# Attention and two expert layers: high parts copied from the operand tiles, loads three heads ahead, transfers and scaling in another order

## The chip, the cores and the metric

One core of a Trainium2 chip. TensorE (PE) multiplies, VectorE (DVE), ScalarE (ACT) and GpSimd (POOL) work element by element, and SyncE (SP) issues all of this kernel's transfers, one after the other. The metric is the time of one execution in microseconds; lower is better.

## The reference

Three stages on float32 data: block-causal attention over 4 batches of 8 heads, 576 positions of 64; a layer g = h cos(h) between two products; and eight experts mixed by a matrix that 8 rounds of row and column scaling make from logits.

```python
scores = scale * np.matmul(q, k.transpose(0, 1, 3, 2))
...
scores = np.where(mask, scores, -1000000000.0)
scores = scores - np.max(scores, axis=-1, keepdims=True)
attn = np.exp(scores)
attn = attn / (np.sum(attn, axis=-1, keepdims=True) + 1e-09)
return np.matmul(attn, v).astype(np.float32)
...
h = x @ w_in
g = h * np.cos(h)
return (g @ w_out).astype(np.float32)
...
for e in range(E):
    h = np.maximum(x @ w1[e], 0.0)
    ye = h @ w2[e]
    out += P[:, e:e + 1] * ye
```

## The kernel before, in words

The order of every engine's queue is the order in which the code is written. `attention()` runs a loop over the 32 heads (batch and head); the two expert stages follow and are not touched.

Precision comes from splitting a float32 value into a high part (rounded to the type fp32r that TensorE reads in one pass) and a low part, the rest. A head i has its K and Q in one tile `st` (K in rows 0 to 63, Q in rows 64 to 127). The scores of a head are sums of two products. One has the high parts: `KA` and `QA` hold them in rows 0 to 63, and in rows 64 to 100 the mask and the row maxima. The other has 128 rows: `KB` holds K's low part and, below it, K's high part; `QB` holds Q's high part and, below it, Q's low part. There are two of each (j = i % 2). The steps for a head:

- `load` fetches `st` (two buffers) by two transfers, `load_v` fetches V by two.
- `hi` copies on ScalarE: K's high part into `KA`, Q's into `QA`, and both into `HI`, a single tile.
- `lo` subtracts on GpSimd: `KB` = `st` - `HI` (both low parts).
- `move_q` and `move_k` are transfers that move halves to the other rows: Q's low part from `KB` to `QB`, Q's high part from `HI` to `QB`, K's high part from `HI` to `KB` (over the low part of Q that the first one has read).
- `peak` (two halves) multiplies high parts for the row maxima, which VectorE reduces out of the PSUM tile `px` (one buffer); `turn` transposes them and `maxima` writes them into `QA`. This is done one head ahead.
- `weights` (four parts) makes the scores and ScalarE their exps; `pv` (five parts) multiplies them with V, into the PSUM tile `o` (one buffer). A column of ones in V gives the sums of the exps.
- `evac` copies `o` out on ScalarE (L338) into one of four tiles (`tla`, `raw`, `tt`), and writes the row of sums to memory (`sums`).
- For each pair of heads e, e + 1: `fetch` reads the sums back as a small tile `sc`, `invert` takes the reciprocal on VectorE and writes it to memory (`inv`), `spread` reads it into `RB` over 64 rows, twice (the transfers tt<-inv), `scale` multiplies on GpSimd, and `x_hi` (ScalarE) and `x_lo` (GpSimd) split the result into the next stage's input.

In 27 heads of 32 (`work`: all but every sixth) five steps of `conv_gen` are put in between, which turn 64-bit weights into float32: a load of 512 KB (`cw`), VectorE's L94, L113, L117 and L124, ScalarE's L100 and L101, GpSimd's L126.

A transfer waits at SyncE until what it reads is made and what it overwrites is free, and all transfers behind it wait as well.

Of the kernel before, what the change touches and what calls it, by code (L numbers as in the profile page):

```python
# [10 lines left out]
F32 = mybir.dt.float32  # L11
# [4 lines left out]
AF = mybir.ActivationFunctionType  # L16
ALU = mybir.AluOpType
# [23 lines left out]
def attention_moe_kernel(ctx: ExitStack, tc: tile.TileContext, qk, v, w_a, gate, w_b, out):  # L41
    nc = tc.nc
# [107 lines left out]
    def attention():  # L150
        with tc.tile_pool(name="at1", bufs=1) as p1, tc.tile_pool(name="at2", bufs=2) as p2, \
# [3 lines left out]
            NH = B * H  # L155
# [8 lines left out]
            HI = p1.tile([128, S], F32R, name="hi")  # L164
# [17 lines left out]
            def some(n):  # L182
                for _ in range(n):
                    next(conv_gen, None)

            def load(i):
                st[i] = p2.tile([128, S], F32, tag="st", name="st")
                nc.sync.dma_start(out=st[i][0:64, :], in_=qk[i][0:64, 1, :])
                nc.sync.dma_start(out=st[i][64:128, :], in_=qk[i][64:128, 0, :])
# [28 lines left out]
                nc.vector.memset(V[1][:, :, 0:D], 0.0)  # L218
                nc.vector.memset(V[1][:, :, 0:1], 1.0)

            def hi(i):
                j = i % 2
                nc.scalar.activation(KA[j][0:64, :], st[i][0:64, :], AF.Copy)
                nc.scalar.activation(QA[j][0:64, 64:640], st[i][64:128, :], AF.Copy)
                nc.scalar.activation(HI, st[i], AF.Copy)  # L225

            def lo(i):

                nc.gpsimd.tensor_tensor(out=KB[i % 2], in0=st[i], in1=HI.bitcast(F32), op=ALU.subtract)  # L229

            def move_q(i):
                j = i % 2
                nc.sync.dma_start(out=QB[j][64:128, :].bitcast(F32), in_=KB[j][64:128, :].bitcast(F32))
                nc.sync.dma_start(out=QB[j][0:64, :].bitcast(F32), in_=HI[64:128, :].bitcast(F32))

            def move_k(i):
                nc.sync.dma_start(out=KB[i % 2][64:128, :].bitcast(F32), in_=HI[0:64, :].bitcast(F32))

            def first_head():

# [9 lines left out]
            def peak(i, u):  # L250

                q, k, nm = QA[i % 2], KA[i % 2], NM[i % 2]
                ps = psx.tile([128, 1024], F32, tag="x", name="px")

                def part(t, k0, n, at):
                    nc.tensor.matmul(ps[:, at:at + n], q[0:68, 128 * t:128 * t + 128], k[0:68, k0:k0 + n],  # L256
                                     start=True, stop=True)

                if u == 0:
                    part(4, 320, 256, 256)  # L260
                    part(3, 0, 448, 0)
                    part(4, 0, 512, 512)
                    found = ((3, 0, 448), (4, 448, 576))
                else:
                    part(1, 0, 256, 0)
                    part(2, 0, 320, 192)
                    part(0, 0, 256, 512)
                    found = ((1, 0, 192), (2, 192, 320), (0, 512, 64))
                for t, at, n in found:
                    nc.vector.tensor_reduce(out=nm[:, 96 + t:97 + t], in_=ps[:, at:at + n], op=ALU.max, axis=AX.X)  # L270
# [42 lines left out]
            def pv(i, c):  # L313
                m = D + 1 if i % 2 == 0 else 2 * D
                if c == 0:
                    ps_o[i] = pso.tile([128, 1024], F32, tag="o", name="o")
                o = ps_o[i][0:m]
                vt = V[i % 2][:, :, 0:m]
                if c == 0:
                    nc.tensor.matmul(o[:, 512:1024], vt[:, 0], EP.pop(i), start=True, stop=True)  # L320
                    nc.tensor.matmul(o[:, 448:512], vt[:, 0], EQ[i][:, 0:64], start=True, stop=True)
                elif c == 1:
                    nc.tensor.matmul(o[:, 576:1024], vt[:, 1], EQ.pop(i)[:, 64:512], start=False, stop=True,
                                     skip_group_check=True)
                elif c == 2:
                    nc.tensor.matmul(o[:, 704:1024], vt[:, 2], ER[i][:, 0:320], start=False, stop=True,
                                     skip_group_check=True)
                elif c == 3:
                    nc.tensor.matmul(o[:, 832:1024], vt[:, 3], ER.pop(i)[:, 320:512], start=False, stop=True,
                                     skip_group_check=True)  # L330
                else:
                    nc.tensor.matmul(o[:, 960:1024], vt[0:64, 4], EC.pop(i), start=False, stop=True,
                                     skip_group_check=True)

            def evac(i):
                m = D + 1 if i % 2 == 0 else 2 * D
                t = RAW[i // 2 % 2][i % 2]
                nc.scalar.activation(t[0:m], ps_o.pop(i)[0:m, 448:1024], AF.Identity, bias=eps[0:m, i % 2:i % 2 + 1])  # L338
                if i % 2 == 0:
                    SUMS[i] = dr.tile([2, S], F32, tag="s", name="sums")  # L340
                s = SUM[i % 2]
                nc.sync.dma_start(out=SUMS[i - i % 2][i % 2:i % 2 + 1, :], in_=t[s:s + 1, :])

            def fetch(e):
                nc.sync.dma_start(out=SC, in_=SUMS.pop(e).rearrange("h (p j) -> p h j", j=8))

            def invert(e):
                nc.vector.reciprocal(out=SC, in_=SC)
                INV[e] = dr.tile([2, S], F32, tag="i", name="inv")
                nc.sync.dma_start(out=INV[e].rearrange("h (p j) -> p h j", j=8), in_=SC)  # L350

            def spread(e):
                d = INV.pop(e)
                for h in range(2):
                    nc.sync.dma_start(out=RB[64 * h:64 * h + 64, :], in_=d[h:h + 1, :].partition_broadcast(64))
# [2 lines left out]
                b, p = divmod(e // 2, NC)  # L358
                return p, slice(b * S, (b + 1) * S)

            def scale(e):
                for h in range(2):
                    r = slice(64 * h, 64 * h + 64)
                    nc.gpsimd.tensor_tensor(out=XF[r, :], in0=RAW[e // 2 % 2][h][r, :], in1=RB[r, :], op=ALU.mult)

            def x_hi(e):
                nc.scalar.activation(xh[:, place(e)[0], place(e)[1]], XF, AF.Copy)

            def x_lo(e):
                p, cols = place(e)  # L370
                nc.gpsimd.tensor_tensor(out=xl[:, p, cols], in0=XF, in1=xh[:, p, cols].bitcast(F32),
                                        op=ALU.subtract)
# [8 lines left out]
            peak(0, 1)  # L381
            turn(0)
            maxima(0)
            hi(1)
            lo(1)
            for i in range(NH):
                nxt, even, odd = i + 1 < NH, i % 2 == 0, i % 2 == 1
                work = i % 6 != 5
                if even and i >= 4:
                    scale(i - 4)  # L390
                if odd and i >= 5:
                    x_lo(i - 5)
                if i:
                    evac(i - 1)
                if nxt:
                    move_q(i + 1)
                if i and nxt:
                    load_v(i + 1)
                if i + 2 < NH:
                    load(i + 2)  # L400
                if nxt:
                    peak(i + 1, 0)
                weights(i, 0)
                weights(i, 1)
                weights(i, 2)
                weights(i, 3)
                if odd and i >= 3:
                    invert(i - 3)
                if work:
                    some(2)  # L410
                if nxt:
                    peak(i + 1, 1)
                pv(i, 0)
                pv(i, 1)
                if nxt:
                    turn(i + 1)
                    maxima(i + 1)
                for c in range(2, 5):
                    pv(i, c)
                if nxt:  # L420
                    move_k(i + 1)
                if even and i >= 2:
                    fetch(i - 2)
                if odd and i >= 3:
                    spread(i - 3)
                if work:
                    some(1)
                if i + 2 < NH:
                    hi(i + 2)
                    lo(i + 2)  # L430
                if work:
                    some(2)
                if even and i >= 4:
                    x_hi(i - 4)
            evac(NH - 1)
            e = NH - 2
            scale(e - 2)
            return conv_gen, {0: lambda: (x_hi(e - 2), fetch(e)),
                              1: lambda: (invert(e), x_lo(e - 2)), 2: lambda: spread(e),
                              4: lambda: (scale(e), x_hi(e)), 5: lambda: x_lo(e)}  # L440

    with tc.manual_schedule():
        conv_gen, leftover = attention()
# [477 lines left out]
```

## Time and profile before

| | us |
|---|---|
| median of 3 runs | 2354.38 (2353.14 to 2354.81) |
| the profiled execution | 2354.91 |
| its span, first to last instruction | 2353.1 |
| TensorE busy | 2202.4 (94%) |
| VectorE, ScalarE, GpSimd busy | 1521.5, 1033.8, 1062.9 |

The shares are averages over the whole span. The attention heads lie in the first 370 us, where the page's slices show TensorE busy for five to seven tenths; behind that nine tenths and more.

### The profile page before, as it was taken

Reading aid. Unit: us, or ns where it says so; the run is one execution under the profiler, and the core shown is the slowest. Engines: PE = TensorE matmul, PEld = TensorE weight load, DVE = VectorE, ACT = ScalarE, POOL = GpSimd, SP = SyncE. Lnnn points to the kernel's source line nnn. Section 1 sums busy time; section 2 is a strip of 40 time slices with the busy share of each in tenths; the row PEclk is TensorE's granted clock in tenths of the full one; section 3 lists DMA queues with packets and bytes.
Section 4 is the critical chain, followed back from the end, with each engine's and each line's share of the span. In section 5 each row is a group of like instructions: output and inputs, shape, how many; then the busy total and the mean of one; then the engine's idle time right before and its main releaser. Section 6 shows DMA issues by size and latency. Waiting matters only on the chain.

```text
span 2353.1 us, 29528 instructions
## 1 busy us (share of the span) xinstructions
PE 2202.4 (94%) x10869; PEld 1945.1 (83%) x10869; DVE 1521.5 (65%) x2442; ACT 1033.8 (44%) x1912; POOL 1062.9 (45%) x897
## 2 busy tenths in 40 slices
PE   5777667999999989999999999999999999999999
PEld 4555456999899878888888888888888888888888
DVE  5445447667666677666667766666667666666665
ACT  4555545555555433343334434433443443344332
POOL 2444437666556434334435533443347444334432
PEclk9778878999999999999999999999999999999999
DMA  4454542000000112112211221221221222122211
GB/s 123 123 134 129 137 123 80 1 1 1 1 1 19 36 54 72 63 63 72 72 61 65 90 71 65 72 72 58 68 72 64 89 72 72 57 70 72 72 56 44
DMA packets 75152, 156.89 MB, mean 67 GB/s; under 512 B 31904, under 2 KB 31904, under 8 KB 75008
## 3 DMA queue, kind: packets, MB, share of 16 engines
q1 hardware_dynamic: 75008, 155.02, 21.5%
q8 instruction: 85, 1.39, 0.2%
q14 instruction: 59, 0.48, 0.1%
HBM read 136.40 MB, written 4.87 MB: 60 GB/s over the span
## 4 chain that ended last, share of the span: by engine, by line
PE 60%; DVE 4%; ACT 1%; issue 0%; DVEq 0%; ACTq 0%
PE acc L449 11%; PE acc L451 11%; PE acc L450 11%; PE hx L451 5%; PE hx L449 5%; PE hx L450 5%; PE hy L449 3%; PE hy L451 3%; PE hy L450 3%; PE hz L449 1%; PE hz L451 1%; PE hz L450 1%; DVE hl L779 1%; DVE wal L551 0%; ACT hh L778 0%; DVE wbl L540 0%
## 5 line engine op out<-in xcount | busy, mean ns | idle before, releaser
L560 POOL TENSOR_TENSOR wv<-stg,wv 128x512 fp32r<-128x512 f32 x190 | 335.5, 1787 | 856.6 <-ACT wv L559 843.1
L449 PE MATMUL acc<-wv,hh 128*128 128x512 f32 x1152 | 456.2, 396 | 0.0
L451 PE MATMUL acc<-wv,hl 128*128 128x512 f32 x1152 | 455.5, 395 | 0.0
L450 PE MATMUL acc<-wv,hh 128*128 128x512 f32 x1152 | 454.5, 394 | 0.0
L807 DVE SCALAR_TENSOR_TENSOR oa<-acc,P,oa 128x512 f32<-128x512 f32 x540 | 378.9, 740 | 4.9 <-PE acc L451 4.3
L778 ACT ACTIVATE hh<-c 128x384 fp32r<-128x384 f32 x288 | 151.2, 525 | 420.0 <-DVE c L863 170.0
L70 POOL TENSOR_TENSOR jl<-raw,jh 128x512 fp32r<-128x512 f32 x190 | 253.2, 1344 | 170.7 <-ACT jh L67 170.6
L779 DVE SCALAR_TENSOR_TENSOR hl<-c,hh 128x384 fp32r<-128x384 f32 x288 | 167.4, 581 | 176.4 <-ACT hh L778 176.4
L451 PEld LDWEIGHTS acc<-wv,hl 128*128 128x128 f32 x1152 | 216.0, 187 | 53.7
L450 PEld LDWEIGHTS acc<-wv,hh 128*128 128x128 f32 x1152 | 215.9, 187 | 44.0
L449 PEld LDWEIGHTS acc<-wv,hh 128*128 128x128 f32 x1152 | 216.1, 188 | 43.2
L857 DVE TENSOR_TENSOR c<-hz,c 128x384 f32<-128x384 f32 x96 | 53.4, 557 | 193.9 <-PE hz L451 193.9
L551 DVE TENSOR_TENSOR wal<-s,wah 128x1024 fp32r<-128x1024 f32 x96 | 172.3, 1794 | 0.0
L847 ACT ACTIVATE c<-hx 128x384 f32<-128x384 f32 x96 | 47.4, 494 | 276.6 <-PE hx L451 276.6
L270 DVE TENSOR_REDUCE nm<-px 128x1 f32<-128x448 f32 (+4 forms) x160 | 69.6, 484 | 148.2 <-PE px L256 148.1
L67 ACT ACTIVATE jh<-raw 128x512 fp32r<-128x512 f32 x192 | 119.4, 623 | 98.8 <-PE acc L450 85.1
L229 POOL TENSOR_TENSOR kb<-st,hi 128x576 fp32r<-128x576 f32 x31 | 48.3, 1558 | 208.2 <-ACT hi L225 164.3
L451 PE MATMUL h<-xh,jl 128*128 128x384 f32 x384 | 131.2, 342 | 10.5 <-POOL jl L70 10.3
L449 PE MATMUL h<-xh,jh 128*128 128x384 f32 x384 | 130.3, 339 | 6.5 <-ACT jh L67 6.3
L660 DVE TENSOR_TENSOR hl<-g,hh 128x384 fp32r<-128x384 f32 x96 | 99.6, 1038 | 56.7 <-ACT hh L658 56.7
L449 PE MATMUL acc<-hh,jh 128*128 128x384 f32 x384 | 129.8, 338 | 5.9 <-DVE xl L678 5.0
L449 PE MATMUL hy<-xh,wah 128*128 128x384 f32 x384 | 129.4, 337 | 3.8 <-DVE c L863 3.7
(211 smaller groups left out, 5311.3 us busy)
## 6 DMA issues: line engine op xcount, KB each, us to landing
stg<-in_w_b_dram SPq DMA_DIRECT2D x192, 512.0 KB
cw<-in_w_a_dram SPq DMA_DIRECT2D x32, 512.0 KB
st<-in_qk_dram SPq DMA_DIRECT2D x64, 144.0 KB
tt<-inv SPq DMA_DIRECT2D x32, 144.0 KB
out_dram<-oa SPq DMA_DIRECT2D x18, 256.0 KB
qb<-kb SPq DMA_DIRECT2D x31, 144.0 KB
qb<-hi SPq DMA_DIRECT2D x31, 144.0 KB
kb<-hi SPq DMA_DIRECT2D x31, 144.0 KB
```

What stands on the lines that cost most here:

```text
L67: nc.scalar.activation(hi, src, AF.Copy)
L70: eng_lo.tensor_tensor(out=lo, in0=src, in1=hi.bitcast(F32), op=ALU.subtract)
L270: nc.vector.tensor_reduce(out=nm[:, 96 + t:97 + t], in_=ps[:, at:at + n], op=ALU.max, axis=AX.X)
L449: nc.tensor.matmul(ps, lh, rh, start=first, stop=False, skip_group_check=go_on)
L450: nc.tensor.matmul(ps, lh, rl, start=False, stop=False, skip_group_check=go_on)
L451: nc.tensor.matmul(ps, ll, rh, start=False, stop=last, skip_group_check=go_on)
L551: eng.tensor_tensor(out=self.al, in0=self.s, in1=self.ah.bitcast(F32), op=ALU.subtract)
L560: eng.tensor_tensor(out=t[:, DM:2 * DM], in0=src, in1=t[:, 0:DM].bitcast(F32), op=ALU.subtract)
L660: nc.vector.tensor_tensor(out=G[n][1], in0=g, in1=G[n][0].bitcast(F32), op=ALU.subtract)
L778: nc.scalar.activation(hh, src, AF.Relu)
L779: nc.vector.scalar_tensor_tensor(out=hl, in0=src, scalar=0.0, in1=hh.bitcast(F32), op0=ALU.max, op1=ALU.subtract)
L807: nc.vector.scalar_tensor_tensor(out=o, in0=acc, scalar=p, in1=o, op0=ALU.mult, op1=ALU.add)
```

## The change

`hi` becomes `hi_q` (ScalarE: `HI`, then `QA`) and `hi_k` (VectorE: `KA`). `move_q` and `move_k` read the high parts from `QA` and `KA` instead of `HI`. `load` runs three heads ahead instead of two and stands behind the second peaks; `hi_q`, `hi_k` and `lo` of head i + 2 stand ahead of the products with V instead of behind them. `move_k` stands ahead of the first peaks, `sums` is parted from `evac`, `give` (the write of `inv`) from `invert`, which now opens an odd head. `scale` does one half in an even and the other in an odd head, and `x_hi` and `x_lo` follow in the odd head.

```diff
--- before.py
+++ after.py
@@ -218,11 +218,12 @@
                 nc.vector.memset(V[1][:, :, 0:D], 0.0)
                 nc.vector.memset(V[1][:, :, 0:1], 1.0)
 
-            def hi(i):
-                j = i % 2
-                nc.scalar.activation(KA[j][0:64, :], st[i][0:64, :], AF.Copy)
-                nc.scalar.activation(QA[j][0:64, 64:640], st[i][64:128, :], AF.Copy)
+            def hi_q(i):
                 nc.scalar.activation(HI, st[i], AF.Copy)
+                nc.scalar.activation(QA[i % 2][0:64, 64:640], st[i][64:128, :], AF.Copy)
+
+            def hi_k(i):
+                nc.vector.tensor_copy(out=KA[i % 2][0:64, :], in_=st[i][0:64, :])
 
             def lo(i):
 
@@ -231,10 +232,10 @@
             def move_q(i):
                 j = i % 2
                 nc.sync.dma_start(out=QB[j][64:128, :].bitcast(F32), in_=KB[j][64:128, :].bitcast(F32))
-                nc.sync.dma_start(out=QB[j][0:64, :].bitcast(F32), in_=HI[64:128, :].bitcast(F32))
+                nc.sync.dma_start(out=QB[j][0:64, :].bitcast(F32), in_=QA[j][0:64, 64:640].bitcast(F32))
 
             def move_k(i):
-                nc.sync.dma_start(out=KB[i % 2][64:128, :].bitcast(F32), in_=HI[0:64, :].bitcast(F32))
+                nc.sync.dma_start(out=KB[i % 2][64:128, :].bitcast(F32), in_=KA[i % 2][0:64, :].bitcast(F32))
 
             def first_head():
 
@@ -336,9 +337,11 @@
                 m = D + 1 if i % 2 == 0 else 2 * D
                 t = RAW[i // 2 % 2][i % 2]
                 nc.scalar.activation(t[0:m], ps_o.pop(i)[0:m, 448:1024], AF.Identity, bias=eps[0:m, i % 2:i % 2 + 1])
+
+            def sums(i):
+                t, s = RAW[i // 2 % 2][i % 2], SUM[i % 2]
                 if i % 2 == 0:
                     SUMS[i] = dr.tile([2, S], F32, tag="s", name="sums")
-                s = SUM[i % 2]
                 nc.sync.dma_start(out=SUMS[i - i % 2][i % 2:i % 2 + 1, :], in_=t[s:s + 1, :])
 
             def fetch(e):
@@ -346,6 +349,8 @@
 
             def invert(e):
                 nc.vector.reciprocal(out=SC, in_=SC)
+
+            def give(e):
                 INV[e] = dr.tile([2, S], F32, tag="i", name="inv")
                 nc.sync.dma_start(out=INV[e].rearrange("h (p j) -> p h j", j=8), in_=SC)
 
@@ -358,10 +363,9 @@
                 b, p = divmod(e // 2, NC)
                 return p, slice(b * S, (b + 1) * S)
 
-            def scale(e):
-                for h in range(2):
-                    r = slice(64 * h, 64 * h + 64)
-                    nc.gpsimd.tensor_tensor(out=XF[r, :], in0=RAW[e // 2 % 2][h][r, :], in1=RB[r, :], op=ALU.mult)
+            def scale(e, h):
+                r = slice(64 * h, 64 * h + 64)
+                nc.gpsimd.tensor_tensor(out=XF[r, :], in0=RAW[e // 2 % 2][h][r, :], in1=RB[r, :], op=ALU.mult)
 
             def x_hi(e):
                 nc.scalar.activation(xh[:, place(e)[0], place(e)[1]], XF, AF.Copy)
@@ -381,35 +385,53 @@
             peak(0, 1)
             turn(0)
             maxima(0)
-            hi(1)
+            hi_q(1)
+            hi_k(1)
             lo(1)
+            load(2)
             for i in range(NH):
                 nxt, even, odd = i + 1 < NH, i % 2 == 0, i % 2 == 1
                 work = i % 6 != 5
-                if even and i >= 4:
-                    scale(i - 4)
-                if odd and i >= 5:
-                    x_lo(i - 5)
+                if odd and i >= 3:
+                    invert(i - 3)
+                if i >= 4:
+                    scale(i - 4 - i % 2, i % 2)
                 if i:
                     evac(i - 1)
                 if nxt:
                     move_q(i + 1)
+                if odd and i >= 3:
+                    give(i - 3)
                 if i and nxt:
                     load_v(i + 1)
-                if i + 2 < NH:
-                    load(i + 2)
+                if i:
+                    sums(i - 1)
                 if nxt:
+                    move_k(i + 1)
                     peak(i + 1, 0)
                 weights(i, 0)
                 weights(i, 1)
                 weights(i, 2)
                 weights(i, 3)
-                if odd and i >= 3:
-                    invert(i - 3)
                 if work:
                     some(2)
                 if nxt:
                     peak(i + 1, 1)
+                if i + 3 < NH:
+                    load(i + 3)
+                if even and i >= 2:
+                    fetch(i - 2)
+                if odd and i >= 3:
+                    spread(i - 3)
+                if i + 2 < NH:
+                    hi_q(i + 2)
+                    hi_k(i + 2)
+                    lo(i + 2)
+                if work:
+                    some(1)
+                if odd and i >= 5:
+                    x_hi(i - 5)
+                    x_lo(i - 5)
                 pv(i, 0)
                 pv(i, 1)
                 if nxt:
@@ -417,27 +439,16 @@
                     maxima(i + 1)
                 for c in range(2, 5):
                     pv(i, c)
-                if nxt:
-                    move_k(i + 1)
-                if even and i >= 2:
-                    fetch(i - 2)
-                if odd and i >= 3:
-                    spread(i - 3)
-                if work:
-                    some(1)
-                if i + 2 < NH:
-                    hi(i + 2)
-                    lo(i + 2)
                 if work:
                     some(2)
-                if even and i >= 4:
-                    x_hi(i - 4)
             evac(NH - 1)
             e = NH - 2
-            scale(e - 2)
-            return conv_gen, {0: lambda: (x_hi(e - 2), fetch(e)),
-                              1: lambda: (invert(e), x_lo(e - 2)), 2: lambda: spread(e),
-                              4: lambda: (scale(e), x_hi(e)), 5: lambda: x_lo(e)}
+            sums(NH - 1)
+            scale(e - 2, 0)
+            scale(e - 2, 1)
+            return conv_gen, {0: lambda: (x_hi(e - 2), fetch(e)), 1: lambda: (invert(e), give(e), x_lo(e - 2)),
+                              2: lambda: spread(e), 4: lambda: (scale(e, 0), scale(e, 1), x_hi(e)),
+                              5: lambda: x_lo(e)}
 
     with tc.manual_schedule():
         conv_gen, leftover = attention()
```

SyncE's queue in one odd head of the steady state (names: `sc8` is the small tile of sums, `st` K and Q of a head, `cw` the weights to convert, `tt_117` the spread reciprocals). Before:

```order
L342 DMA sums_1562<-tla_119 1x576
L233 DMA qb0_106<-kb0_108 64x576
L234 DMA qb0_106<-hi_110 64x576
L194 DMA v0_114<-in_v_dram 128x4x64
L195 DMA v0_114<-in_v_dram 64x64
L188 DMA st_1568<-in_qk_dram 64x576
L189 DMA st_1568<-in_qk_dram 64x576
L350 DMA inv_1602<-sc8_122 72x2x8
L89 DMA cw_121<-in_w_a_dram 128x1024
L237 DMA kb0_108<-hi_110 64x576
L355 DMA tt_117<-inv_1602 64x576 x2
```

With the change, from the read of the sums at the end of the even head to the end of the odd one:

```order
L348 DMA sc8_122<-sums_1429 72x2x8
L234 DMA qb0_106<-kb0_108 64x576
L235 DMA qb0_106<-qa0_102 64x576
L355 DMA inv_1566<-sc8_122 72x2x8
L194 DMA v0_114<-in_v_dram 128x4x64
L195 DMA v0_114<-in_v_dram 64x64
L345 DMA sums_1570<-tla_119 1x576
L238 DMA kb0_108<-ka0_104 64x576
L89 DMA cw_121<-in_w_a_dram 128x1024
L188 DMA st_1614<-in_qk_dram 64x576
L189 DMA st_1614<-in_qk_dram 64x576
L360 DMA tt_117<-inv_1566 64x576 x2
```

The row of sums and the move into `kb` have changed places with the loads of `st`: `kb` now stands ahead of `cw`, the loads behind it; `inv` stands between the moves of Q and the loads of V, three transfers behind the read `sc8` on which it depends.

ScalarE's queue from one evacuation to the next, before:

```order
L338 ACTIVATE tt_116<-o_1324,eps_70 128x576
L294 ACTIVATE ep_1365<-sp_1362 128x512
L300 ACTIVATE eq_1372<-sq_1367 128x512
L306 ACTIVATE er_1379<-sr_1374 128x512
L311 ACTIVATE ec_1384<-sc_1381 64x64
L100 ACTIVATE tla_119<-tla_119,e_max_74 128x512
L101 ACTIVATE tla_119<-tla_119,e_all_76 128x512
L223 ACTIVATE ka0_104<-st_1353 64x576
L224 ACTIVATE qa0_102<-st_1353 64x576
L225 ACTIVATE hi_110<-st_1353 128x576
L367 ACTIVATE xh_78<-tt_118 128x576
L338 ACTIVATE tla_119<-o_1397,eps_70 65x576
```

With the change:

```order
L339 ACTIVATE tt_116<-o_1336,eps_70 128x576
L295 ACTIVATE ep_1365<-sp_1362 128x512
L301 ACTIVATE eq_1372<-sq_1367 128x512
L307 ACTIVATE er_1379<-sr_1374 128x512
L312 ACTIVATE ec_1384<-sc_1381 64x64
L222 ACTIVATE hi_110<-st_1323 128x576
L223 ACTIVATE qa0_102<-st_1323 64x576
L100 ACTIVATE tla_119<-tla_119,e_max_74 128x512
L101 ACTIVATE tla_119<-tla_119,e_all_76 128x512
L339 ACTIVATE tla_119<-o_1407,eps_70 65x576
```

The copy into `KA` is gone, the copies into `hi` and `qa` stand straight behind the four exps, and `xh` is in every odd head instead of every even one.

VectorE's queue around the reciprocal, before:

```order
L117 SCALAR_TENSOR_TENSOR raw_1115<-cw_121,raw_1115 128x512
L270 TENSOR_REDUCE nm0_111<-px_1130 128x1 x2
L348 RECIPROCAL sc8_122<-sc8_122 72x16
L124 SCALAR_TENSOR_TENSOR tla_119<-cw_121,tla_119 128x512
L94 TENSOR_SCALAR tla_119<-cw_121 128x512
L270 TENSOR_REDUCE nm0_111<-px_1167 128x1 x3
L278 TENSOR_TENSOR qa0_102<-pt_1178,diag_113 5x640
L113 TENSOR_SCALAR raw_1115<-cw_121 128x512
L117 SCALAR_TENSOR_TENSOR raw_1115<-cw_121,raw_1115 128x512
```

With the change:

```order
L113 TENSOR_SCALAR raw_1117<-cw_121 128x512
L117 SCALAR_TENSOR_TENSOR raw_1117<-cw_121,raw_1117 128x512
L351 RECIPROCAL sc8_122<-sc8_122 72x16
L271 TENSOR_REDUCE nm0_111<-px_1132 128x1 x2
L124 SCALAR_TENSOR_TENSOR tla_119<-cw_121,tla_119 128x512
L94 TENSOR_SCALAR tla_119<-cw_121 128x512
L271 TENSOR_REDUCE nm0_111<-px_1166 128x1 x3
L226 CAST ka1_105<-st_1097 64x576
L279 TENSOR_TENSOR qa0_102<-pt_1190,diag_113 5x640
L113 TENSOR_SCALAR raw_1117<-cw_121 128x512
```

The reciprocal has moved ahead of the two reductions of the first peaks, and the cast into `ka` stands between the reductions of the second peaks and the product that writes the maxima.

## Rows read from the trace of the kernel before

**Rows 1.** Windows: stretch, us, busy PE, PEld, DVE, ACT, POOL; clock, DMA share, GB/s.

```profile
23.53:353.69 330.16, 235.91 (x902) 167.55 (x902) 148.50 (x285) 168.95 (x294) 132.01 (x92) 0.80 0.49 129
...
373.50:455.00 81.50, 73.29 (x393) 70.68 (x392) 62.05 (x93) 45.50 (x79) 61.50 (x43) 0.96 0.10 30
```

**Rows 2.** Timeline of ScalarE, first and thirtieth evacuation: start, length, engine, line.

```profile
23.53 0.72 ACT L338 ACTIVATE tla<-o,eps 65x576 f32<-65x576 f32 x1
...
353.69 0.72 ACT L338 ACTIVATE raw<-o,eps 128x576 f32<-128x576 f32 x1
```

**Rows 3.** Waits of the engines from 23.53 to 353.69: total us, times, longest.

```profile
ACT ka L223 <- DMA st<-in_qk_dram: 71.2, 29, 4.1
...
ACT hi L225 <- DMA kb<-hi: 39.4, 17, 3.9
```

**Rows 4.** Waits of the transfer queue in the same stretch.

```profile
SPq L342 <- ACT tla L338: 83.6, 15, 8.6
```

**Rows 5.** Timeline of one head with a load of weights.

```profile
216.09 0.72 ACT L338 ACTIVATE raw<-o,eps 128x576 f32<-128x576 f32 x1
...
216.83 0.22 SPq L342 DMA_DIRECT2D sums<-raw  x1
...
217.71 0.48 SPq L233 DMA_DIRECT2D qb<-kb  x1
...
222.09 0.48 SPq L237 DMA_DIRECT2D kb<-hi  x1
222.63 0.55 SPq L345 DMA_DIRECT2D sc<-sums  x1
...
226.66 0.68 ACT L225 ACTIVATE hi<-st 128x576 fp32r<-128x576 f32 x1 [2.07 <-DMA kb<-hi]
...
227.82 0.73 ACT L338 ACTIVATE tla<-o,eps 65x576 f32<-65x576 f32 x1
```

**Rows 6.** Timeline of the head before it, which has no load of weights.

```profile
213.16 0.48 SPq L237 DMA_DIRECT2D kb<-hi  x1
...
215.50 0.69 ACT L225 ACTIVATE hi<-st 128x576 fp32r<-128x576 f32 x1
```

**Rows 7.** Timeline of the first head: GpSimd's subtraction and VectorE's two copies.

```profile
7.82 1.40 POOL L247 TENSOR_TENSOR qb<-st,hi 64x576 fp32r<-64x576 f32 x1
...
8.14 1.39 DVE L242 CAST ka<-st 64x576 fp32r<-64x576 f32 x1
...
9.56 0.46 DVE L243 CAST qa<-st 64x576 fp32r<-64x576 f32 x1
```

**Rows 8.** Timeline of SyncE in the next head, which has inv and tt.

```profile
229.70 0.49 SPq L233 DMA_DIRECT2D qb<-kb  x1
...
234.50 0.49 SPq L237 DMA_DIRECT2D kb<-hi  x1
235.82 1.24 SPq L355 DMA_DIRECT2D tt<-inv  x2
```

**Rows 9.** Timeline of SyncE and VectorE: a read of the sums behind a load of weights.

```profile
357.78 0.54 SPq L89 DMA_DIRECT2D cw<-in_w_a_dram  x1
358.41 0.46 SPq L237 DMA_DIRECT2D kb<-hi  x1
358.96 0.51 SPq L345 DMA_DIRECT2D sc<-sums  x1
...
362.94 0.25 DVE L348 RECIPROCAL sc<-sc 72x16 f32<-72x16 f32 x1 [0.40 <-DMA sc<-sums]
```

**Rows 10.** Issues of the page: the sizes of the loads.

```profile
cw<-in_w_a_dram SPq DMA_DIRECT2D x32, 512.0 KB
st<-in_qk_dram SPq DMA_DIRECT2D x64, 144.0 KB
```

**Rows 11.** Window of the head from 353.69 to 360.75, columns as in rows 1.

```profile
353.69:360.75 7.06, 7.02 (x30) 4.96 (x28) 5.52 (x9) 4.64 (x9) 6.70 (x5) 0.76 0.67 160
```

**Rows 12.** one conversion step of VectorE (tile tla): count, ns min/median/max, first and last start.

```profile
L94 DVE TENSOR_SCALAR tla<-cw x30: 408/422/1646, 18.6 to 393.0; 128x512 int32<-128x512 int32 x30
```

## The prediction

> **What bounds the kernel now.** I read the windows by stage first [rows 1]. The 32 heads fill the first 370 us of 2353. In them TensorE is 71% busy (235.9 of 330.2 us) at a granted clock of 0.80; behind them, in the first expert stage, it is 90% busy at 0.96. The change touches the heads alone, and the order of TensorE's own instructions is the same, so the question is the time from one head to the next. The evacuation of a head's output (L338) marks the heads: the first starts at 23.53, the thirtieth at 353.69 [rows 2], so 330.16 / 29 = **11.38 us a head**. No engine is that busy: by the same window a head costs TensorE 8.1, ScalarE 5.8, VectorE 5.1 and GpSimd 4.6 us. So the heads wait on a loop, and the waits name it [rows 3]: ScalarE's copy into HI waits for the transfer kb<-hi, and its first copy for the load of st. The queue of transfers waits 83.6 us for the evacuations of the even heads alone [rows 4].
>
> The loop in one head, in order of time [rows 5]: the evacuation at 216.09 releases sums at 216.83; behind it SyncE issues qb, qb, v, v, st, st, cw, and at 222.09 kb<-hi. HI may be overwritten only once that transfer has read it: the copy starts at 226.66, 4.6 us later. The copy of xh and the next evacuation (227.82) stand behind it on ScalarE. Sum: 0.74 to sums, 0.88 to the first qb, 4.4 to kb, 4.6 until kb landed, 1.15 to the evacuation = 11.7 us. Where a head has no weight to convert, no cw stands ahead of kb, which then frees HI after 2.3 us [rows 6]. So a cw ahead costs a transfer 2.3 us.
>
> **The change part by part.**
> *The source of the moves.* qb and kb are now read from QA and KA, so nothing waits for kb to overwrite HI: only GpSimd's subtraction reads HI. The 4.6 us leave the loop. The new writes of KA and QA wait for transfers issued a head earlier, and for scores that stand ahead of them anyway.
> *Loads three heads ahead, high parts behind the exps.* st is loaded a head before it is wanted; its wait (71 us [rows 3]) goes. ScalarE runs two copies for three.
> *The K copy on VectorE.* It saves ScalarE 0.68 us a head. The trace has such a copy twice: 1.39 us while GpSimd runs and 0.46 us alone [rows 7]. I take 0.9; both are below what VectorE has free, so it costs nothing by itself. The Trainium skill ("SBUF — State Buffer", Who interferes with whom) says that a VectorE copy in its two-port mode and GpSimd lock each other out for a whole instruction; the two rows agree, and by it the copy would be worth 1.39 us, and the denser stage would stretch VectorE's other work too (a rival, below).
> *Scaling over two heads, x_hi and x_lo later.* Same work, in smaller pieces. GpSimd's 4.6 us and ScalarE's 5.1 us (5.8 less 0.68) cover it in a head of 7 us or more.
> *The order of transfers.* This decides what is next. SyncE issues one transfer after the other. From the rows, a head that ends in sc takes 0.24 + 0.1 for sums and 217.71 to 223.18 for the rest, 5.8 us; a head with inv and tt takes 0.34, then 229.70 to 234.99, then 1.24 + 0.05, 6.9 us [rows 5, 8]. So **12.7 us of issuing for two heads**, and the change keeps all of it. Two waits come on top.
>
> 1. The read of the sums (sc) now stands behind cw and two st, last in its head, and the reciprocal with its inv is asked for at the very start of the next one, behind two qb. In the trace sc was issued 1.18 us after a cw with one kb between, and the reciprocal could start 3.98 us after the issue [rows 9]. Now 0.74 us more pass after cw (the two st), and one transfer of 144 KB more is ahead: by 2.3 us for cw's 512 KB [rows 10] that is 0.65. So sc lands after 3.9. With the reciprocal (0.25 [rows 9]) SyncE could issue inv 4.2 us after sc; sc and two qb fill 1.8. It waits **2.4 us in every second head**, and v, v, sums, kb, cw, st, tt all stand behind.
> 2. kb must wait until the first qb has read KB. Between them stand qb, v, v, sums: 2.7 us of issue. A qb with nothing ahead lands in 2.3; behind cw, two st and two tt it is later: at 2.3 us per 512 KB those need 2.3 + 4 x 0.65 = 4.9 us and 3.25 of issue have passed, so 3.95, a wait of 1.25. The other bound is nothing. I take **0.8 once in two heads**; where inv waits, qb has long landed.
>
> 12.7 + 2.4 + 0.8 = 15.9 us for two heads. In one pair of three the odd head has no cw: 0.5 less issue, and the next qb doesn't wait, 0.8. Mean 15.5, or **7.7 us a head by SyncE alone**.
>
> TensorE is next. The one head near the end that had no load to wait for took 7.06 us with TensorE busy for 7.02 of them at a clock of 0.76 [rows 11]: 14.1 for two. In the odd head the reciprocal is first in VectorE's queue, and the first row maxima, which free the PSUM that the second peaks need, stand behind it; TensorE stops there for some 1 to 3 us. So 15.1 to 17.1 by that chain. VectorE's 5.1 and 0.9, with some more locking, is 6 to 7.5. Three chains this close don't line up in order, so I add 0.3 us to SyncE's 7.7: **8.0 us a head** (7.4 to 8.6: the landing of sc from 3.0 to 5.0 us, kb's wait from nothing to 1.25, TensorE's stop from 1 to 3).
>
> 29 heads x (11.38 - 8.0) = 98.0 us. The start (23.5 us) and what follows 353.69 stay as they are: the last head's chain there is the same. The profiled execution took 2354.91 us (span 2353.1 and 1.8 around it): 2354.91 - 98.0 = 2256.9. The median of the three runs is 0.5 lower, so **2256 us**, in the likeliest case 2239 to 2274.
>
> **The rivals.**
> *TensorE paces.* If sc lands within the 1.8 us of the two qb, or SyncE's issues run faster, SyncE needs 6.35 us a head and TensorE's 7.06 decides: 29 x 4.32 = 125, 2229 us; a fuller stage at a higher clock would go lower still, to 6.6 and 2216. For it: TensorE has no other new wait. Against: [rows 9] have sc at 4 us. 0.20.
> *VectorE and GpSimd collide.* The mechanism is the lock of [rows 7]. One conversion step took 0.42 us by the median and 1.65 at most [rows 12]. With the K copy there are five such instructions a head; if each met GpSimd they would cost about 1.0 us more each, VectorE 5.1 + 0.46 + 4.9 = 10.5 us. Three quarters of that is 9.25 a head: 29 x 2.13 = 62, 2293 us. Against: GpSimd's 4.6 us are 57% of 8, and a meeting costs on the average half an instruction. The Trainium skill's page "SBUF — State Buffer" would expect it. 0.17.
> *Nothing is gained.* If the loop had a second wait just as long behind HI's. The rows show one candidate, the wait for st, and the change removes that too. 0.02.
> *Slower.* The reciprocal at the front of VectorE's queue closes a loop over two heads: sums, kb, cw, st, st, sc (2.8 us of issue), sc's landing 3.9, the reciprocal 0.25, and then what is left of a head up to the evacuation that the next sums wait for, at most a whole one (7.06): 14 us for two heads, against 22.8 now. It decides from a landing of 12.7 us. At 14 us two heads take 24.1: 29 x 0.67 = 19 us slower, 2374. Only transfers piling up would do it; the 16 engines are now 0.49 busy [rows 1], 0.70 at 8 us a head. 0.04.
>
> **How the numbers follow.** The likeliest case has 0.57. The range takes in the first rival and most of the second: 2222 to 2294 us; beyond it lie the last two, a quarter of the collisions and TensorE at a still higher clock. A measurement of this kernel tells 0.2% (4.7 us) from no change. Faster 0.94, same 0.02, slower 0.04.
>
> **What would show it.** Evacuations some 8 us apart, in pairs: a shorter head, then a longer one. No wait of HI's copy for kb<-ka, none for st. SyncE's inv waiting some 2 us for the reciprocal, and that for sc; kb waiting about 1 us for qb. TensorE's clock above 0.80 and its busy share near 90%. If inv doesn't wait, step 1 is wrong and TensorE should pace; if VectorE's conversion rows have means above 1.2 us, the lock does; if sc lands later than 5 us, transfers crowd.

## The result and the profile after

The changed kernel takes **2266.47 us** (median of 4 runs, 2263.46 to 2268.85), the kernel before 2353.76 in runs beside it: a ratio of **0.9629, interval 0.9613 to 0.9646**. The forecast was 2256 (2222 to 2294).

ScalarE's timeline has the first and the thirtieth evacuation (L339 now) here:

```profile
25.42 0.74 ACT L339 ACTIVATE tla<-o,eps 65x576 f32<-65x576 f32 x1 [0.38 <-PE o L333]
...
266.09 0.74 ACT L339 ACTIVATE raw<-o,eps 128x576 f32<-128x576 f32 x1 [2.67 <-PE o L333]
```

Beside [rows 2]: (266.09 - 25.42) / 29 = **8.30 us a head** where it was 11.38. That is 29 x 3.08 = 89.3 us; the start takes 1.9 us longer, and what follows the thirtieth evacuation is as long as before (2265.8 - 266.09 = 1999.7 against 2353.1 - 353.69 = 1999.4). The whole gain lies in the pace of the heads.

The window of these heads (stretch, its length, busy us of PE, PEld, DVE, ACT and POOL, clock, DMA share, GB/s):

```profile
25.42:266.09 240.67, 200.82 (x900) 137.80 (x900) 191.96 (x316) 155.10 (x264) 134.11 (x92) 0.91 0.68 177
```

Against the first of [rows 1]: TensorE 83% busy for 71%, at a clock of 0.91 for 0.80; VectorE 80% for 45%; the transfers' engines 0.68 for 0.49.

The waits of the engines in it (us in total, times, longest), and those of the transfer queue:

```profile
POOL tt L368 <- DMA tt<-inv: 43.7, 13, 4.8
...
PE px L257 <- DVE nm L271: 35.6, 17, 4.4
...
DVE sc L351 <- DMA sc<-sums: 11.8, 9, 3.6
...
ACT hi L222 <- DMA st<-in_qk_dram: 8.9, 9, 1.8
```

```profile
SPq L355 <- DVE sc L351: 28.3, 14, 3.4
SPq L238 <- DMA qb<-kb: 14.5, 13, 2.0
SPq L234 <- POOL kb L230: 7.9, 12, 1.4
```

The wait of the copy into HI for kb [rows 3] is gone, and the wait for st has shrunk from 71 to 9 us. In their place inv waits for the reciprocal, 2.0 us on the mean in every second head, kb waits 1.1 us for qb in 13 heads, and TensorE stops 2.1 us on the mean at the second peaks in 17 heads. One such odd head, the timeline of SyncE, VectorE and TensorE (start, length, engine, line):

```profile
140.54 0.50 SPq L348 DMA_DIRECT2D sc<-sums  x1
...
143.84 0.25 DVE L351 RECIPROCAL sc<-sc 72x16 f32<-72x16 f32 x1 [0.27 <-DMA sc<-sums]
144.12 0.33 SPq L355 DMA_DIRECT2D inv<-sc  x1
144.12 1.29 DVE L271 TENSOR_REDUCE nm<-px 128x1 f32<-128x448 f32 x2
...
145.56 1.03 PE L257 MATMUL px<-ka,qa 68*128 68x256 f32 x3 [2.92 <-DVE nm L271]
...
146.39 1.91 PE L321 MATMUL o<-ep,v 128*128 128x512 f32 x2
```

sc is issued at 140.54; the reciprocal, the reductions behind it and TensorE's second peaks all follow its landing, and inv with them. VectorE had stood idle for sc for only 0.27 us here: its conversions ahead of the reciprocal ran until 143.58. Of the 14 reciprocals in the window nine waited for sc, 11.8 us in all; the other five came straight behind the conversions. After the stop of 2.9 us the value products run at the lower of TensorE's two clocks, 1.91 us where the same line took 1.02 in a head without such a stop.

### The profile page after: what moved, and what is told of

Read it like the earlier page. It is cut to its first block, busy times and chain, and to the rows that moved or that the text cites. A ratio compares the mean times of both kernels' runs of the same rounds, so it can differ in the third digit from the quotient of the medians.

```text
span 2265.8 us, 29649 instructions
## 1 busy us (share of the span) xinstructions
PE 2169.0 (96%) x10869; PEld 1918.4 (85%) x10869; DVE 1565.3 (69%) x2473; ACT 1020.2 (45%) x1881; POOL 1063.4 (47%) x897
## 4 chain that ended last, share of the span: by engine, by line
PE 62%; DVE 4%; ACT 1%; issue 0%; DVEq 0%; ACTq 0%
PE acc L460 11%; PE acc L462 11%; PE acc L461 11%; PE hx L462 5%; PE hx L460 5%; PE hx L461 5%; PE hy L460 3%; PE hy L462 3%; PE hy L461 3%; PE hz L462 1%; PE hz L461 1%; PE hz L460 1%; DVE hl L790 1%; ACT hh L789 1%; DVE wal L562 1%; DVE wbl L551 0%
## 5 line engine op out<-in xcount | busy, mean ns | idle before, releaser
L462 PE MATMUL hy<-xh,wal 128*128 128x384 f32 x384 | 129.0, 336 | 2.8 <-DVE wal L562 2.8
L461 PE MATMUL h<-xl,jh 128*128 128x384 f32 x384 | 130.8, 341 | 0.0
```

Of the source, the lines that this page charges most:

```text
L461: nc.tensor.matmul(ps, lh, rl, start=False, stop=False, skip_group_check=go_on)
L462: nc.tensor.matmul(ps, ll, rh, start=False, stop=last, skip_group_check=go_on)
```

## The experiments

"us a head" is (thirtieth less first evacuation) / 29 in each kernel's own trace. Ratios are to the kernel before on the same chip; beside these runs it took 2351.78 to 2353.76 us (medians), so two medians of different chips compare to some 2 us.

| kernel | median us | ratio (interval) | us a head |
|---|---|---|---|
| before | 2354.38 | | 11.38 |
| the change | 2266.47 | 0.9629 (0.9613 to 0.9646) | 8.30 |
| b_source | 2298.39 | 0.9773 (0.9759 to 0.9788) | 9.42 |
| b_load3 | 2351.29 | 0.9998 (0.9988 to 1.0007) | 11.28 |
| b_kb_early | 2296.70 | 0.9767 (0.9752 to 0.9781) | 9.33 |
| b_source_load3 | 2292.41 | 0.9745 (0.9730 to 0.9759) | 9.21 |
| b_kb_early_load3 | 2290.44 | 0.9734 (0.9717 to 0.9750) | 9.08 |
| b3_kb_early | 2266.27 | 0.9627 (0.9613 to 0.9641) | 8.24 |
| a_hi | 2269.43 | 0.9640 (0.9625 to 0.9654) | 8.29 |
| a_k_scalar | 2264.44 | 0.9619 (0.9605 to 0.9633) | 8.32 |
| a_inv_later | 2247.98 | 0.9556 (0.9540 to 0.9572) | 7.73 |
| a_inv_k_scalar | 2241.25 | 0.9520 (0.9504 to 0.9535) | 7.53 |
| a_loads_first | 2253.19 | 0.9584 (0.9568 to 0.9600) | 7.92 |
| a_qb_first | 2248.49 | 0.9551 (0.9536 to 0.9565) | 7.57 |

### One part alone, in the kernel before

**b_source.**

```diff
-                nc.sync.dma_start(out=QB[j][0:64, :].bitcast(F32), in_=HI[64:128, :].bitcast(F32))
+                nc.sync.dma_start(out=QB[j][0:64, :].bitcast(F32), in_=QA[j][0:64, 64:640].bitcast(F32))
...
-                nc.sync.dma_start(out=KB[i % 2][64:128, :].bitcast(F32), in_=HI[0:64, :].bitcast(F32))
+                nc.sync.dma_start(out=KB[i % 2][64:128, :].bitcast(F32), in_=KA[i % 2][0:64, :].bitcast(F32))
```

> The kernel before with one edit: the moves into qb and kb read the high parts from QA and KA, nothing else. Theory (the copy into HI waits for kb to land, 4.6 us in heads with a load of weights, and that wait closes the loop): HI's wait goes to nothing, the wait for st ends the loop instead, 9.5 us a head where it was 11.9 and 8.4 as before where there is no load of weights; 29 heads x 2.1 us = about 60 us, 2285 to 2305 us. Rival (the new order of the transfers or the earlier loads made the gain): under 10 us, above 2344 us.

As the theory had it: HI's wait is gone, and 54 us with it. What ends the loop instead is only in part the wait for st, of which 28.6 us in 16 heads are left; the exps of the first scores now wait 42.8 us for TensorE, which the expectation didn't have.

**b_load3.**

```diff
-                if i + 2 < NH:
-                    load(i + 2)
+                if i + 3 < NH:
+                    load(i + 3)
```

(and `load(2)` ahead of the loop)

> The kernel before with loads three heads ahead, in the place where they stood; the moves still read HI. Theory: no change beyond 5 us (2349 to 2359 us): the wait of the first copy for st goes from 71 us to near nothing and comes back as a longer wait of the copy into HI for kb, since the loop through HI is as long as before. Rival (the loads are what was late): 71 us of waits go, about 2285 us.

Nothing, as the theory had it. The waits of its heads show where the 71 us for st went (the first line is of the kernel before, beside [rows 3]):

```profile
ACT hi L225 <- issue: 20.0, 7, 3.3
...
ACT hi L225 <- issue: 87.0, 17, 6.2
...
ACT hi L225 <- DMA kb<-hi: 51.6, 11, 6.6
```

The copy into HI now waits 51.6 us for kb and 87.0 for what the profile doesn't name, where it had 39.4 [rows 3] and 20.0. A wait that stood ahead of a longer one was not the bound.

**b_kb_early.** Only `move_k(i + 1)` is moved, from behind the value products to ahead of the first peaks.

```diff
                 if nxt:
+                    move_k(i + 1)
                     peak(i + 1, 0)
...
-                if nxt:
-                    move_k(i + 1)
                 if even and i >= 2:
                     fetch(i - 2)
```

> The kernel before with one line moved: the move into kb stands ahead of the load of weights instead of behind it. The moves still read HI, loads are two heads ahead. Theory (what closed the loop was kb's landing behind 512 KB, 4.6 us instead of 2.3; either of the two ways out, another source or an earlier kb, is enough): every head becomes like those without a load of weights, 8.4 to 8.8 us; 29 heads x 2.6 to 3.0 us, 2266 to 2280 us. Rival (HI's wait and the wait for st must both be out of the loop): 9.4 us a head or more as with the new source alone, 2295 us or more.

A miss: 55 us, as much as the new source, and not 80. The expectation took the 8.4 us of heads without a load of weights for all. Those are odd heads, and an even head has the copy into xh between HI and the evacuation as well: in the trace odd heads take 8.9 and even ones 9.8 us on the mean. What closes the loop is the load of st, for which the first copy waits 70.6 us in 29 heads; one even head:

```profile
163.10 0.72 ACT L338 ACTIVATE tt<-o,eps 128x576 f32<-128x576 f32 x1
...
167.77 0.60 SPq L189 DMA_DIRECT2D st<-in_qk_dram  x1
...
170.00 0.69 ACT L223 ACTIVATE ka<-st 64x576 fp32r<-64x576 f32 x1 [2.87 <-DMA st<-in_qk_dram]
170.96 0.68 ACT L224 ACTIVATE qa<-st 64x576 fp32r<-64x576 f32 x1 [0.27 <-DMA st<-in_qk_dram]
171.66 0.69 ACT L225 ACTIVATE hi<-st 128x576 fp32r<-128x576 f32 x1
172.25 0.67 ACT L367 ACTIVATE xh<-tt 128x576 fp32r<-128x576 f32 x1
172.83 0.72 ACT L338 ACTIVATE tla<-o,eps 65x576 f32<-65x576 f32 x1
```

### Two and three parts together, in the kernel before

**b_source_load3** has the edits of b_source and b_load3.

> The kernel before with both edits, and nothing of the new order, the scaling or the K copy on VectorE. Theory (both waits together were the loop): about the time of the full change. kb behind a load of weights lands 4.6 us after its issue, 10 us after the evacuation two heads earlier, and the scores, exps and value products take some 6 us more: 16 us for two heads, 8.1 a head; 2255 to 2280 us. Rival (the order of the transfers and the high parts behind the exps carry a good part of the gain): 2290 us or more.

A miss: of the change's 87 us only 60 are there. HI and st are out of the way, and the next is the scores, which wait for kb, still issued behind the load of weights: the exps of the first scores wait 52.2 us in 28 heads for TensorE, and TensorE's weight load for the scores 24.3 us for what the profile doesn't name, where kb is the operand on its way. One head, from kb's issue to the first product of the scores, 4.8 us (the median of 30 heads is 4.8 too):

```profile
204.12 0.48 SPq L237 DMA_DIRECT2D kb<-ka  x1
...
208.91 0.52 PE L286 MATMUL sp<-qb,kb 128*128 128x512 f32 x1 [1.28 <-issue]
```

**b_kb_early_load3** has those of b_kb_early and b_load3.

> The kernel before with two edits: the move into kb ahead of the load of weights, and loads three heads ahead. The moves still read HI. Alone the first gave 9.3 us a head (what was left was the wait of the first copy for st) and the second nothing. Theory (two waits close the loop one after the other, HI's for a late kb and the first copy's for st; the source of the moves is one of two ways out of the first): both gone, 8.2 to 8.5 us a head, 2262 to 2272 us, as with all three edits (2266). Rival (HI's wait still costs when the source is left): 2280 us or more.

A miss too, and the rival was right. With st out of the way HI's wait for kb is back at 72.0 us in 23 heads, although kb lands 2.9 us after its issue:

```profile
158.75 0.54 SPq L237 DMA_DIRECT2D kb<-hi  x1
...
161.69 0.69 ACT L225 ACTIVATE hi<-st 128x576 fp32r<-128x576 f32 x1 [1.84 <-DMA kb<-hi]
```

**b3_kb_early** has all three.

> The kernel before with the new sources, loads three heads ahead and one part of the new order: the move into kb stands ahead of the load of weights, behind the loads. Theory (what the two edits alone lacked, 2292 against 2266, is kb landing 4.6 us after a load of weights, for which TensorE's scores wait): the scores' wait goes and 20 us or more come back, 2262 to 2274 us. Rival (it is the high parts made behind the exps, or the scaling): under 6 us, 2286 us or more.

As the theory had it by the time, and as much as the whole change: 2266.27 against 2266.47. The scores now start 3.0 us after kb's issue (median 3.1):

```profile
169.73 0.54 SPq L237 DMA_DIRECT2D kb<-ka  x1
...
172.77 0.47 PE L286 MATMUL sp<-qb,kb 128*128 128x512 f32 x1 [1.81 <-DMA kb<-ka]
```

Their wait is shorter, not gone: the exps of the first scores still wait 33.4 us in 25 heads. So three edits make the gain together, each behind the last: one loop through HI, one of nearly the same length through st, and behind them the scores' wait for kb. The new source and the early kb without the earlier loads were not run. What is left of the change (the places of the high parts, of the sums and of inv, the halves of the scaling, the K copy on VectorE) adds nothing that can be measured as a whole. That doesn't put each part at nothing: a_inv_later, below, shows that the place of the reciprocal and inv costs the change some 18 us, so the others may gain about as much.

### One part undone, in the change

**a_hi**: the two lines of b_source the other way round.

> The changed kernel with one part undone: the moves into qb and kb read the high parts from HI again. Theory (HI's wait for kb is what the new source takes away, and it costs less here because kb now stands ahead of the load of weights): the copy into HI waits some 2 us in each head for kb, ScalarE's queue behind it comes late; 8.6 to 9.0 us a head where the change has 8.3: 2275 to 2287 us. Rival (with kb issued early the source no longer matters): within 5 us of the change's 2266.

A miss. The copy into HI waits 82.2 us in 28 heads for kb, and yet the time is that of the change:

```profile
ACT hi L222 <- DMA kb<-hi: 82.2, 28, 3.9
...
SPq L234 <- POOL kb L230: 47.8, 29, 6.2
```

In exchange inv waits 7.2 us for the reciprocal instead of 28.3, and TensorE 13.6 at the second peaks for the reductions instead of 35.6. As I read it, later high parts make GpSimd's subtraction late, the queue waits for that ahead of qb (47.8 us for 7.9), and sc has time to land: one wait stands in the other's place. In the change's order the new source is one of two ways to the same pace. Whether it matters once inv stands later was not run.

**a_k_scalar**: the copy into KA on ScalarE.

```diff
-                nc.vector.tensor_copy(out=KA[i % 2][0:64, :], in_=st[i][0:64, :])
+                nc.scalar.activation(KA[i % 2][0:64, :], st[i][0:64, :], AF.Copy)
```

> The changed kernel with the copy into KA on ScalarE again. Theory (the late read of the sums paces, VectorE stands still for it anyway): within 6 us of the change, 2260 to 2272 us. Rival (VectorE, locked against GpSimd, paces; the copy takes 0.96 us of it in a head): up to 28 us faster, 2238 to 2255 us.

No difference. VectorE, with 24.8 us less to do, now stands still for sc ahead of all 14 reciprocals (16.5 us, where it was nine and 11.8), and inv waits as long as before (30.8 for 28.3). So the load of VectorE, the lock against GpSimd with it, doesn't pace the change.

### The late read of the sums

**a_inv_later**: the reciprocal behind the reductions of the first peaks, inv between the sums and kb.

```diff
-                if odd and i >= 3:
-                    invert(i - 3)
                 if i >= 4:
...
-                if odd and i >= 3:
-                    give(i - 3)
...
                 if nxt:
-                    move_k(i + 1)
                     peak(i + 1, 0)
+                if odd and i >= 3:
+                    invert(i - 3)
+                    give(i - 3)
+                if nxt:
+                    move_k(i + 1)
```

> The changed kernel with the reciprocal behind the reductions of the first peaks and its write inv behind the sums, ahead of kb. Theory (sc lands too late for a reciprocal at the head's start; SyncE waits 2.0 us in every second head and TensorE stops for about 2 us, after which the clock falls): inv's wait falls below 0.8 us, TensorE's stops at the second peaks are gone, its clock in the heads rises to 0.97 or more, 7.2 to 7.6 us a head instead of 8.3: 20 to 32 us faster than the change, 2235 to 2247 us. Rival (VectorE with its conversions locked against GpSimd paces, 81% busy): under 6 us, 2260 us or more.

18.5 us faster than the change by the medians, 17 by the ratios, a little short of what was expected, and the mechanism in part as expected: inv's wait falls from 28.3 to 9.6 us (13 times, 0.74 each), the stops at the second peaks from 35.6 to 23.6. The edit shortens both at once; what each was worth isn't told apart. The stops that remain, and the window of the heads:

```profile
PE px L257 <- DVE sc L351: 15.4, 10, 2.5
PE px L257 <- DVE nm L271: 8.2, 8, 2.1
...
25.08:249.30 224.22, 196.21 (x900) 135.69 (x900) 193.03 (x316) 155.20 (x264) 134.62 (x92) 0.94 0.73 189
```

TensorE's clock is 0.94, not 0.97. VectorE is 86% busy, and 13 of the 14 reciprocals now follow its own work without a wait for sc. Its conversion steps are long where GpSimd runs (line, tile, shape, count, busy us and mean ns):

```profile
L117 DVE SCALAR_TENSOR_TENSOR raw<-cw,raw 128x512 f32<-128x512 uint16 x25 | 33.9, 1357 | 0.9
L226 DVE CAST ka<-st 64x576 fp32r<-64x576 f32 x29 | 29.4, 1013 | 0.0
```

L117 took 0.69 us in all heads before. Here all of its 15 runs of more than 0.9 us overlap an instruction of GpSimd, and none of the ten short ones does. This is the lock that the Trainium skill describes ("SBUF — State Buffer", Who interferes with whom), and [rows 7] agree. One step further the collision rival is part of the pace, as the next run shows.

**a_inv_k_scalar**: that, and the copy into KA on ScalarE.

> Both edits: reciprocal and inv later, and the copy into KA on ScalarE. There the wait for the sums is out of the way and VectorE was 86% busy, its conversion steps 1.7 us long where GpSimd runs. Theory (with the sums out of the way VectorE is next): half of its 0.96 us a head or more comes back, 12 to 24 us faster than the later reciprocal alone (2248): 2224 to 2236 us. Rival (SyncE or TensorE is next): under 5 us, 2243 us or more.

Between the two: 6.7 us come back. It is the fastest kernel of the study, 2241.25 us, 25 below the change. TensorE is 88% busy, at 0.97.

**a_loads_first**: that, and `load(i + 3)` ahead of `move_k(i + 1)`, so that kb finds qb landed.

> The changed kernel with reciprocal and inv later, the K copy on ScalarE, and the loads of st ahead of kb instead of behind the load of weights. Theory (SyncE's queue paces; kb waits 1.2 us in every second head for qb, with the loads between them it finds qb landed): kb's wait near nothing, 0.4 to 0.6 us a head, 2224 to 2231 us. Rival (TensorE, VectorE and the lock pace by now): within 4 us of 2241.

A miss, 12 us slower than without. kb's wait is gone, but the load of st now waits for the load of weights, with which it shares no data; it is the eighth transfer behind it. Other waits grew as well: VectorE's first conversion step waits 21.3 us for the weights in nine heads, and the exps of the first scores 32.2 us where it was 14.9. Which of them costs the 12 us wasn't tested.

```profile
SPq L188 <- DMA cw<-in_w_a_dram: 15.8, 9, 2.2
```

**a_qb_first**: a_inv_k_scalar with the moves of Q ahead of tt in odd heads, and the first half of the scaling behind the subtraction in even ones.

> The fastest so far (reciprocal and inv later, K copy on ScalarE: 2241 us) with the moves of Q ahead of the spread tt at the end of odd heads, and the first half of the scaling behind GpSimd's subtraction instead of ahead of it. Theory (SyncE's queue paces at 7.5 us a head, 1.2 us of every second one is kb's wait for qb behind tt): kb's wait falls below 0.4 us in the pair and GpSimd's wait for tt at the front of its queue goes; 7.1 to 7.3 us a head, 2228 to 2236 us. Rival (TensorE, 6.6 us busy a head, and VectorE pace): within 4 us of 2241.

A miss for both, 7 us slower. kb's wait for qb fell from 16.8 to 2.6 us and GpSimd's wait for tt is no longer among the long ones, as meant, but the pace of the profiled execution, the fastest of four (2243.60 to 2250.12), stayed at 7.57 us. In it inv waits 15.5 us for the reciprocal, where it was 10.1. So kb's wait for qb doesn't set the pace at 7.5 us; what does isn't settled.

## Why the prediction was right, step by step

*The loop through HI.* Right, shown by b_source and b_load3. That the wait for st was a second loop was foreseen in "nothing is gained"; that a third lay behind both (scores waiting for a kb that is behind the weights) was not, and the change happened to remove it too. My text credited the first two with the whole, and b_source_load3 shows that they give 60 of the 87 us: that the rest came as well was luck.

*The next bound.* Right: SyncE's inv waits for a reciprocal, which waits for sc in nine of 14 heads. Step 1 had 2.4 us in every second head, it is 2.0; the reciprocal started 3.3 us after sc's issue in the head shown and 4.1 in the next such head, where sc's landing was foreseen at 3.9. Step 2 had 0.8, it is 1.1. a_inv_later takes two thirds of the first away and gains 18.5 us.

*TensorE's stop.* Foreseen as 1 to 3 us, measured 2.1 on the mean and 4.4 at most. Its after-effect, the lower clock for the value products that follow, was in no term. The 7.06 us of a head without a stop were read at a clock of 0.76 [rows 11]; the change's even heads took 6.0 to 7.2 at 1.00. TensorE's busy share, foreseen near 90%, is 83%.

*The sum.* 8.0 us a head was foreseen, 8.30 measured: 29 x 0.30 = 8.7 us of the 10 that are missing; the longer start is 1.9. The mis-sized term is the allowance for chains that don't line up, 0.3 us where 0.6 was needed on top of SyncE's 7.7. What fills it isn't shown; there are two candidates. One is the lower clock: by the windows of the next paragraph it makes TensorE 8 x 2.33 = 18.6 us busier in the 29 heads, and in six heads the load of v waits for the late value products (5.1 us). But a_hi has the same pace at a clock of 0.96. The other is GpSimd. It was put at nothing because its busy time is short; but at the head of its queue it waits 3.4 us for tt in 13 heads, its subtraction comes late, and qb waits for that 7.9 us in 12 heads. Neither was taken away by itself in this kernel.

*The pairs.* A shorter head and then a longer one were foreseen. In the trace the long one comes strongest in about every second pair. From the third head on the odd heads are of two kinds: eight of 10.6 to 14.1 us, in which TensorE's granted clock is 0.73 to 0.85 and TensorE 8.1 to 9.7 us busy, and six of 7.4 to 8.4 us at 1.00, 6.4 to 6.5 us busy. One of each, the head of the timeline above and the next odd one (columns as in the window above):

```profile
139.69:152.49 12.80, 9.71 (x32) 6.24 (x32) 9.49 (x15) 5.96 (x10) 7.59 (x6) 0.73 0.76 208
158.56:166.93 8.37, 6.38 (x32) 4.63 (x32) 6.21 (x10) 4.53 (x8) 4.39 (x4) 1.00 0.55 135
```

The same products, 32 in the trace of either, take TensorE 3.3 us more. TensorE's stops were 1.9 to 4.4 us in the eight and 1.0 to 2.0 in the six. So the long heads are those in which the clock is down after the stop; why that comes in about every second pair stays open.

*The rivals.* The lock has longer rows than before (means: L113 0.82, L117 1.14, the K copy 0.95 us), but a_k_scalar shows that VectorE's load doesn't pace the change. "Slower" fell: the reciprocal starts 3.2 to 4.9 us after sc's issue, far from 12.7.

## What to carry to other kernels

Count a loop's waits one behind the other: a one-line edit that takes the longest away may show half of what it is worth, and one that takes a wait away in front of a longer one shows nothing. Where transfers are issued from one queue, keep small ones that others wait for ahead of a large load, and ask for what a read brings only when its landing time has passed. An operation that waits at the head of an in-order queue holds up what stands behind it, however short it is: here the reciprocal of 0.25 us, with the row maxima and TensorE's second peaks behind it.

## What the runs showed of the hardware beyond that

After a stop of 2.9 us TensorE ran at its lower clock: the same two value products then took 1.91 us for 1.02. The stop's length alone doesn't tell: in two heads the clock fell after 1.92 us, in another it stayed at 1.00 after 1.99. In a_loads_first a load of 512 KB issued at 139.09 let VectorE go at 145.90, 6.8 us later, with tt, qb, v and sums issued behind it. A transfer behind such a load had landed 4.6 us after its own issue [rows 5]. Whether the load is slowed by what follows it or by the two loads of st and the kb issued just ahead of it, no run tells apart.

```profile
139.09 0.54 SPq L89 DMA_DIRECT2D cw<-in_w_a_dram  x1
...
145.90 0.43 DVE L94 TENSOR_SCALAR tla<-cw 128x512 int32<-128x512 int32 x1 [2.46 <-DMA cw<-in_w_a_dram]
```
